# Half of the output weights split later, in places of the first expert's weights, and two more places for experts' tiles

## The chip, the cores and the metric

The kernel runs on one core of a Trainium2 chip (trn2). The metric is the device time of one execution in microseconds, lower is better. The time before is the median of three runs, 391.73 us (389.76 to 392.42).

## What is computed

Three stages follow one another, all in fp32 at the boundary.

```python
# retention: 8 batches, 8 heads, 576 positions, 64 wide; D[i,j] = gamma_h ** (i-j) for i >= j, else 0
x = (q @ k.T / 8 * D) @ v                       # -> x: 4608 tokens x 512
# soft mixture of experts: 8 experts of 4 slots; phi 512 x 32, w1[e] 512 x 1024, w2[e] 1024 x 512
logits = x @ phi
slots = softmax(logits, over tokens).T @ x      # 32 x 512
out_e = relu(slots[e] @ w1[e]) @ w2[e]          # 8 experts, 4 slots each
x = softmax(logits, over slots) @ out           # 4608 x 512
# bilinear block: m1, m2 512 x 1024; w3 1024 x 1024; w_out 1024 x 512
y = ((x @ m1) * (x @ m2)) @ w3 @ w_out          # 4608 x 512
```

The weights m1, m2, w3 and w_out come as float64 and are turned into fp32 on the chip; the rest is float32.

## The kernel before, in words

**The order of the work is written out by hand.** Each engine and each queue executes its instructions in the order in which the program emits them. All large loads go out on the sync queue (SP), in that order: a load whose place is still being read holds up every load that is written behind it.

**Attention** (0 to about 162 us) runs over 36 units of 128 tokens. Each unit multiplies queries, keys and values, scales, and turns the result for the expert logits. Beside it the loop loads what comes later. At three points of each unit `pace` lets one waiting load go, tied to an instruction of TensorE. The list of waiting loads holds key, value and query tiles and one `next_load` per unit (two in units 10, 14, 18, 22, 26). `next_load` takes the next *piece* of the float64 weights, if one of the four raw buffers is free, and otherwise calls `load_expert`, which takes the next expert tile if a place is free, and else does nothing. In the last nine units three more `load_expert` calls stand in each unit, and the places of keys, values and queries come free one after the other.

**Pieces.** There are 40 pieces of 512 KB: 8 of w_out (interleaved with the first of m1), 16 of m1 and m2, 16 of w3. Converting one takes two operations on ScalarE, three on VectorE and one addition on GpSimd (`conv_list`, `add`). A piece of w_out or w3 is then split into two fp32r numbers, high and low: a copy on ScalarE (`copy`, line 528) and a subtraction on GpSimd (`sub`, line 533). `nsplit` counts the splits. Values of w_out and w3 wait for the split in three buffers (`vals`).

**Products of w3 and w_out** (`emit_Ws`, line 564) are 64 groups of three 128x512 matmuls. Eight groups accumulate one block of 128 rows of w3 @ w_out; each group reads one of the eight split w_out pieces (`k8`), all of them in one tile, `wop`, of 32 KB per partition. The groups are used as filler for TensorE: three before the first expert, then as many at each of the four steps of an expert as a formula by step allows (line 956), 58 by the second step of the last one.

**Experts** (about 172 to 246 us). An expert's weights are eight tiles of 512 KB: four for the first layer (`emit_l1`, line 602), four for the second (`emit_l2`, line 622). Between the layers ScalarE applies the relu (607) and VectorE transposes (615). The places of a layer's four tiles go to the list `free` behind its matmuls, and `load_expert` (583) takes from it. In the first six experts one place per expert is kept for a finished block of w3 @ w_out (`wplaces`). With the experts' places and the ones that were in the attention 19 tiles are asked for before the first layer of the first expert: one place (`ew0`) is there for experts from the start, the other 18 come free during the attention's end. At the first expert `ew0` and one further place go to the softmax over slots.

**Behind the experts** come the slots' outputs through m1 and m2, the products of pairs of slots (written over the split w_out), the matmul of these with w3 @ w_out, and then nine token blocks with 12 matmuls for each 128 tokens and the stores.

Of the kernel before, what the change touches and what calls it, by code (L numbers as in the profile page):

```python
# [10 lines left out]
F32R = mybir.dt.float32r  # L11
# [5 lines left out]
ALU = mybir.AluOpType  # L17
# [14 lines left out]
def retention_softmoe_bilinear(  # L32
# [15 lines left out]
    nc = tc.nc  # L48
    const = ctx.enter_context(tc.tile_pool(name="const", bufs=1))
# [20 lines left out]
    bank = [*b2(scores), one, output[:, 512:1024], state, output[:, 0:512], *b2(pair)]  # L70
# [10 lines left out]
    block = lambda t, i, n=1: t[:, 1024 * i:1024 * (i + n)]  # L81

    mw_sb = const.tile([128, 8192], F32, name="mw_sb")
    wop = const.tile([128, 8192], F32R, name="wop")
    w3p = const.tile([128, 3072], F32R, name="w3p")

    NRAW = 4
# [10 lines left out]
    def place(tag, name=None, dt=F32):  # L98
        t = new("place", name or tag, 1024, dt, tag=tag)
        all_places.append((t, tag))  # L100
        return t

    def tag_of(t):
        return next(g for x, g in all_places if x is t)

    both = lambda t: [t[:, o:o + 512] for o in (0, 512)]
# [12 lines left out]
    xt_places = [place(f"xts{i}") for i in range(3)]  # L119
    xg_places, p_places, s_place, kt_place = [place("xg0"), place("xg1")], [place("pm0"), place("pm1")], place("st"), place("kt")  # L120
# [5 lines left out]
    qb = [place(f"q{i}") for i in range(QBUF)]  # L126
    vb = [place(f"v{i}") for i in range(VBUF)]
    rb = [place(f"kr{i}") for i in range(RBUF)]
    kb = [place(f"k{i}") for i in range(KBUF)]
    ring = [place("ew0")]  # L130


    lo, hi = slice(0, 64), slice(64, 128)
# [324 lines left out]


    pieces = []  # L460
    woh, wol = wop[:, 0:4096], wop[:, 4096:8192]
    for i in range(8):
        pieces.append(wo[:, 512 * i:512 * i + 512])
    for i in range(16):
# [2 lines left out]
        pieces.append(w3[i // 2][:, 512 * (i % 2):512 * (i % 2) + 512])  # L467
    N3 = 24
    turn = [j for i in range(8) for j in (i, 8 + i)] + list(range(16, len(pieces)))
    nth = lambda j: j if j < 8 else j - 16  # L470

    def value(j):
        t = mw_sb[:, 512 * (j - 8):] if 8 <= j < N3 else vals[:, 512 * (nth(j) % 3):]
        return t[:, 0:512]

# [37 lines left out]

    def high_low(j):
        if j < 8:
            return woh[:, 512 * j:512 * j + 512], wol[:, 512 * j:512 * j + 512]
        t = block(w3p, (j - N3) % 3)
        return t[:, 0:512], t[:, 512:1024]

    def add(i):  # L520
        j = turn[i]
        ti = value(j).bitcast(I32)
        nc.gpsimd.tensor_tensor(out=ti, in0=ti, in1=parts[i % 2].bitcast(I32), op=ALU.add)  # L523
        if not 8 <= j < N3:
            copies.append(j)

    def copy(j):
# [16 lines left out]
    nsplit, nW = [0], [0]  # L544
# [3 lines left out]
    wplaces = xg_places[:]  # L548
# [3 lines left out]
    def emit_Ws(n, lag=1):  # L552
        for _ in range(n):
            i, k = divmod(nW[0], 4)
            if i == 16 or nsplit[0] < min(9 + i + lag, 24):
                return
            nW[0] += 1
            ps = bank[(5, 2)[i // 2 % 2]]
            b = block(w3p, i % 3)
            ah, al = (b[:, o + 128 * k:o + 128 * k + 128] for o in (0, 512))  # L560
            k8 = 4 * (i % 2) + k
            bh, bl = (t[:, 512 * k8:512 * k8 + 512] for t in (woh, wol))
            for part, (x, y) in enumerate(((ah, bh), (ah, bl), (al, bh))):
                nc.tensor.matmul(out=ps, lhsT=x, rhs=y, start=(k8 == 0 and part == 0), stop=(k8 == 7 and part == 2))  # L564
            if k8 == 7:
                evicts.append(lambda cb=i // 2, ps=ps: evict(cb, ps))
# [9 lines left out]
    ew, free = [], []  # L576
# [41 lines left out]
    def emit_l2(e):  # L618
        ht = ht_of[e]
        for cb in range(8):  # L620
            qd = cb % 4
            nc.tensor.matmul(  # L622
                out=bank[4][32 * qd:32 * qd + 32], lhsT=ht[:, 32 * cb:32 * cb + 32], rhs=ew[8 * e + 4 + cb // 2][:, 512 * (cb % 2):512 * (cb % 2) + 512],
                start=(e == 0 and cb < 4), stop=(e == 7 and cb >= 4), skip_group_check=True,
            )
        free.extend(ew[8 * e + 4:8 * e + 8])
# [28 lines left out]
    with tc.manual_schedule():  # L655
# [69 lines left out]
        output_factors(0)  # L725
        output_factors(1)

        free.extend(ring)
        came, TWICE, PACED = [], (10, 14, 18, 22, 26), 3

        def can_conv():
            if nconv[0] == nl[0]:
                return False
            j = turn[nconv[0]]
            return 8 <= j < N3 or nth(j) < nsplit[0] + 3

        def next_conv(u):
            if not conv_ops and nconv[0] < len(came) and came[nconv[0]] <= u and can_conv():
# [11 lines left out]
        for u in range(NU):  # L750
# [32 lines left out]
            if u + 1 < NU:  # L783
                emit_state(u + 1)
                n = pairs_in_order.index(units[u + 1][0]) if units[u + 1][1] else 0
# [52 lines left out]
        run(subs)  # L838
        run_copies()
        run(adds)  # L840
        free.extend([*p_places, s_place])
        load_expert(4)
        load_pieces()
        close_pool("psum")
# [19 lines left out]
        emit_dT(T)  # L864
        emit_xtr(NU - 2)
        emit_xtr(NU - 1, nc.vector.tensor_copy)
        free.extend(xt_places)
        load_expert(7)
        nc.tensor.matmul(out=bank[1][:, 0:1], lhsT=nrow.rearrange("p g s -> p (g s)"), rhs=ident[0:1, 0:1], start=True, stop=True)
        negm = tmp.tile([128, 1], F32, tag="negm", name="negm")  # L870
# [12 lines left out]
        for k in range(4):  # L883
            for a, b in ((lo, 64), (hi, 0)) if k % 2 else ((slice(0, 128), 0),):
                n = a.stop - a.start
# [7 lines left out]
            out=sme, in0=sT.rearrange("p k (e j) -> p e k j", j=4),  # L893
            in1=rzs.rearrange("p x (e j) -> p e x j", j=4).to_broadcast([128, 8, 4, 4]), op=ALU.mult,
# [25 lines left out]
            run(evicts)  # L920


        nsoft = [0]

        def soft():
# [12 lines left out]
        for e in range(NE):  # L938
            load_expert(8)
            last = emit_l1(e)  # L940
            if e == NE - 1:
                store_expt(last)
            if e == 0:

                free[:] = [t for t in free if not any(t is x for x in ring)]
                second = tag_of(free.pop(0))
                etp = [place("ew0", "et0"), place(second, "et1")]
                L["et"] = [t.rearrange("p (t n) -> p t n", n=128) for t in etp]
                L["soft"] = [etp[1][:, o:o + 128].rearrange("p (g s) -> p g s", g=4) for o in (512, 640)]
            for t in range(4):  # L950
                tick()
                if t == 1:
                    emit_turned(e)
                load_expert(8)
                step = 4 * e + t + 1
                emit_Ws(max(0, (min(5, 3 + step), min(7, 1 + step), min(55, 7 + (step - 8) * 48 // 20))[min(e, 2)] - nW[0]))
                if e == NE - 1 and t == 1:
                    emit_Ws(3, 0)
                if t == 2:
                    emit_l2(e)  # L960
                    if len(wplaces) < 8:
                        wplaces.append(free.pop(0))
                    load_expert(8)
                while e < NE - 1 and nsoft[0] <= (4 * e + t) * 18 // 28:
                    soft()
                convert(3)
# [12 lines left out]

        m4 = lambda t: t.rearrange("p (m n) -> p m n", m=4)  # L980
        two = lambda tag, n: [t[:, o:o + 512] for t in [place(tag, n, F32R)] for o in (0, 512)]
        left = [t for t in map(tag_of, qb + vb + rb + kb + p_places + [s_place, kt_place] + xt_places) if t not in [second, *map(tag_of, wplaces)]]
        cs2 = two(left[0], "cs")
        for i in range(2):
            L["cc"].append(tuple(zip(*[two(t, f"cc{i}{m}") for m, t in enumerate(left[4 * i + 1:4 * i + 5])])) + (cs2[i],))
# [1 line left out]
        gs, phl = two(left[10], "gs")  # L987
        phl = phl.rearrange("p (c x s) -> p c x s", c=8, x=2)
        y16 = [vals[:, 512 * i:512 * i + 512] for i in range(2)]
        ph, pl = (wop[:, 4096 * i:4096 * i + 4096].rearrange("p (c n) -> p c n", c=8) for i in range(2))  # L990
        ab = [t.rearrange("p (c s) -> p c s", c=8) for t in (mw_sb[:, 3584:4096], parts[0])]
        af = bank[4].rearrange("p (c s) -> p c s", c=8)
        for x in range(2):
            mw = mw_sb[:, 4096 * x:4096 * x + 4096].rearrange("p (k f) -> p k f", k=4)
            for k in range(4):
                for g in range(4):
                    nc.tensor.matmul(
                        out=bank[7 - x][32 * g:32 * g + 32, 0:256], lhsT=sot[:, k],
# [35 lines left out]
        def pairs(cb):  # L1034
            if cb > 7:
                return
            t1, t2 = sums(cb), ptmp[cb % 2][1]
            v = nc.vector
            for a, b in ((0, 4), (4, 8), (8, 16)) if cb == 0 else ((0, 16),):
                c = max(a, 1)  # L1040
                v.tensor_tensor(out=t2[:, c - 1:b - 1], in0=base(ab[1], cb, b - c), in1=win(af, cb, c, b - c), op=ALU.mult)
                v.tensor_tensor(out=t1[:, a:b], in0=base(af, cb, b - a), in1=win(ab[1], cb, a, b - a), op=ALU.mult)
                v.tensor_tensor(out=t1[:, c:b], in0=t1[:, c:b], in1=t2[:, c - 1:b - 1], op=ALU.add)
                nc.scalar.copy(out=ph[:, cb, 32 * a:32 * b], in_=t1[:, a:b].rearrange("p a b -> p (a b)"))

        def pairs_low(cb):
            t1 = sums(cb).rearrange("p a b -> p (a b)")
            nc.vector.tensor_tensor(out=pl[:, cb, 0:512], in0=t1, in1=ph[:, cb, 0:512], op=ALU.subtract)

        GB = (0, 1, 5, 3)  # L1050

        def g_mm(cb, m, parts):
            sl = slice(128 * m, 128 * m + 128)
            for i in parts:
                a, b = ((ph, wh), (ph, wl), (pl, wh))[i]
                nc.tensor.matmul(
                    out=bank[GB[m]], lhsT=a[:, cb, sl], rhs=b[cb],
                    start=(cb == 0 and i == 0), stop=(cb == 7 and i == 2), skip_group_check=True,
                )

# [154 lines left out]
```

## Time and profile before

| | |
|---|---|
| median of three runs | 391.73 us (389.76 to 392.42) |
| the profiled execution's own time | 393.84 us |
| its span | 392.1 us |
| TensorE matmul busy | 375.4 us (96%) |
| TensorE weight loads busy | 284.9 us (73%) |
| VectorE busy | 257.4 us (66%) |
| ScalarE busy | 199.0 us (51%) |
| GpSimd busy | 172.6 us (44%) |
| moved by the sync queue's transfers | 107.85 MB, 86.4% of 16 engines' span |
| read from memory | 97.41 MB |

Matmuls are pipelined: a 128x512 matmul is shown with about 0.40 us, but in a row of them the next one starts long before the one ahead ends. So "busy" says that TensorE has something in flight, and not that it works at its best. PE is TensorE's matmul row, PEld its weight-load row, DVE VectorE, ACT ScalarE, POOL GpSimd, SPq the sync queue. Tiles of experts' weights are named by the place that they are in (`k`, `kr`, `q`, `v`, `xts`, `ew`), so `xts<-in_ew` is a load of expert weights into a place that held something else before. Where several instructions stand in one row, its duration is from the first start to the last end.

### The profile page before, as it was taken

How to read it: one execution, taken by the hardware profiler on the slowest of the kernel's cores; microseconds unless marked ns; L12 is line 12 of the kernel's file. 1: busy time of each engine (PE TensorE's matmuls, PEld its weight loads, DVE VectorE, ACT ScalarE, POOL GpSimd, SP SyncE). 2: the span in 40 equal slices, each digit the busy share in tenths (PEclk: the TensorE clock that was granted, in tenths of full speed). 3: DMA queues.
4: the chain of work that ended last, by engine and by line, in shares of the span. 5: the costliest groups of instructions: out<-in, count | busy, mean ns of one | idle time of the engine just before them, and what ended most of it. 6: DMA issues, size and time to landing. Idle time of an engine off the chain costs nothing.

```text
span 392.1 us, 10958 instructions
## 1 busy us (share of the span) xinstructions
PE 375.4 (96%) x4447; PEld 284.9 (73%) x4447; DVE 257.4 (66%) x432; ACT 199.0 (51%) x424; POOL 172.6 (44%) x158
## 2 busy tenths in 40 slices
PE   6999999999997999799999999999999999999996
PEld 3888787878876897564666664678688777788774
DVE  4648999899896889555477963399766445355500
ACT  2347696788675787423364532234445353544432
POOL 2733765675464436202345652127544334552420
PEclk9999999999999999999999999999999999999999
DMA  7999899899988999999999999692359989998634
GB/s 241 335 331 333 301 365 323 252 375 376 291 274 313 305 324 331 325 397 371 410 409 408 410 407 389 153 210 39 82 114 207 232 221 227 235 222 210 158 89 103
DMA packets 48211, 108.75 MB, mean 277 GB/s; under 512 B 7584, under 2 KB 10016, under 8 KB 48160
## 3 DMA queue, kind: packets, MB, share of 16 engines
q1 hardware_dynamic: 47008, 107.85, 86.4%
q8 instruction: 35, 0.57, 0.6%
q10 hardware_dynamic: 1152, 0.20, 0.3%
q14 instruction: 16, 0.13, 0.1%
HBM read 97.41 MB, written 10.62 MB: 275 GB/s over the span
## 4 chain that ended last, share of the span: by engine, by line
PE 74%; DVE 14%; DMA 8%; issue 2%; ACT 1%; POOL 1%; ACTq 0%; POOLq 0%; DVEq 0%
PE bank L564 10%; PE bank L1131 9%; PE bank L1133 8%; PE bank L1132 8%; PE output L282 6%; PE scores L253 5%; DMA kr<-in_v 4%; PE output L316 4%; PE bank L622 3%; PE bank L602 3%; PE state L296 3%; DMA v<-in_ew 2%; PE one L356 2%; PE bank L1122 2%; PE pair L215 2%; DVE vals L497 2%
## 5 line engine op out<-in xcount | busy, mean ns | idle before, releaser
L646 POOL TENSOR_TENSOR cc<-mw_sb,cc 128x512 fp32r<-128x512 f32 x36 | 46.0, 1297 | 56.5 <-ACT cc L645 56.5
L523 POOL TENSOR_TENSOR vals<-vals,msb 128x512 int32<-128x512 int32 x24 | 30.8, 1284 | 46.7 <-DVE vals L497 44.5
L564 PE MATMUL bank<-wop,w3p 128*128 128x512 f32 x192 | 50.0, 404 | 0.0
L263 DVE TENSOR_TENSOR pm<-scores,msb 128x1024 f32<-128x1024 f32 x31 | 37.8, 1220 | 15.0 <-PE scores L253 14.8
L564 PEld LDWEIGHTS bank<-wop,w3p 128*128 128x128 f32 x192 | 34.4, 188 | 14.4 <-issue 7.1
L645 ACT CAST cc<-mw_sb 128x512 fp32r<-128x512 f32 x36 | 22.2, 616 | 43.6 <-DVE mw_sb L644 34.8
L1131 PE MATMUL bank<-w3p,cc 128*128 128x512 f32 x108 | 43.1, 399 | 0.0
L1133 PE MATMUL bank<-w3p,cc 128*128 128x512 f32 x108 | 42.1, 390 | 0.0
L1132 PE MATMUL bank<-w3p,cc 128*128 128x512 f32 x108 | 42.0, 389 | 0.0
L253 PE MATMUL scores<-q,kt 64*128 64x128 f32 x496 | 36.6, 285 | 2.0 <-issue 2.0
L644 DVE TENSOR_TENSOR mw_sb<-lga,raw 128x512 f32<-128x512 f32 x32 | 29.3, 955 | 12.3 <-POOL cc L646 12.1
L282 PE MATMUL output<-pm,v 128*64 128x128 f32 x512 | 36.1, 284 | 1.0 <-issue 1.0
L523 POOL TENSOR_TENSOR mw_sb<-mw_sb,msb 128x512 int32<-128x512 int32 x16 | 20.4, 1276 | 33.9 <-DVE mw_sb L497 25.7
L1135 ACT ACTIVATE mw_sb<-bank,rz 128x512 f32<-128x512 f32 x36 | 24.7, 685 | 19.0 <-PE bank L1133 9.4
L253 PEld LDWEIGHTS scores<-q,kt 64*128 64x128 f32 x496 | 30.3, 187 | 4.8 <-issue 2.9
L533 POOL TENSOR_TENSOR w3p<-vals,w3p 128x512 fp32r<-128x512 f32 x16 | 21.2, 1326 | 28.7 <-ACT w3p L528 19.8
L282 PEld LDWEIGHTS output<-pm,v 128*64 128x64 f32 x512 | 28.1, 139 | 6.1 <-issue 4.9
L220 ACT COPY kt<-pair 128x512 f32<-128x512 f32 x26 | 15.2, 585 | 29.1 <-PE pair L219 29.1
L504 ACT ACTIVATE msb<-raw 128x512 int32<-128x512 uint32 x40 | 27.8, 696 | 0.0
L192 POOL TENSOR_TENSOR k<-kr,msb 128x512 f32<-128x512 f32 (+1 forms) x30 | 25.9, 886 | 3.9 <-DMA kr<-in_v 3.9
L1131 PEld LDWEIGHTS bank<-w3p,cc 128*128 128x128 f32 x108 | 20.3, 188 | 7.1 <-issue 2.9
L503 DVE TENSOR_SCALAR vals<-vals 128x512 f32<-128x512 f32 x24 | 18.5, 772 | 7.6 <-ACT vals L502 7.6
(226 smaller groups left out, 775.3 us busy)
## 6 DMA issues: line engine op xcount, KB each, us to landing
q<-in_q SPq DMA_DIRECT2D x20, 512.0 KB, 6.5
raw<-expt SPq DMA_DIRECT2D x36, 256.0 KB, 4.4
kr<-in_v SPq DMA_DIRECT2D x16, 512.0 KB, 6.0
v<-in_v SPq DMA_DIRECT2D x16, 512.0 KB, 6.8
raw<-in_m SPq DMA_DIRECT2D x16, 512.0 KB, 6.2
raw<-in_w SPq DMA_DIRECT2D x16, 512.0 KB, 6.1
out_x<-mw_sb SPq DMA_DIRECT2D x64, 128.0 KB, 2.4
q<-in_ew SPq DMA_DIRECT2D x14, 512.0 KB, 10.1
```

What stands on the lines that cost most here:

```text
L192: (nc.vector if first else nc.gpsimd).tensor_tensor(out=Ks[:, :, 0:m, h], in0=K[:, 1 - h, :, 0:m], in1=ktab(c, h)[:, 0:m].unsqueeze(1).uns ...
L253: last = nc.tensor.matmul(out=ps[:, p], lhsT=ktb[u % 2][a, p], rhs=Q[a, :, x, p], start=True, stop=True)
L263: nc.vector.tensor_tensor(out=p_places[u % 2].rearrange("p (g t) -> p g t", g=8), in0=(pair if u == 1 else scores).rearrange("p (g t) -> p ...
L282: last = nc.tensor.matmul(out=xt_view(p)[side(p, h)], lhsT=v_tile(u)[:, 1 - h, x, p], rhs=p_main(u)[:, h, p], start=(block_of(u) == 0 and ...
L504: lambda: nc.scalar.activation(out=p.bitcast(I32), in_=lo, func=ACTF.Copy, scale=2.0 ** -29),
L523: nc.gpsimd.tensor_tensor(out=ti, in0=ti, in1=parts[i % 2].bitcast(I32), op=ALU.add)
L564: nc.tensor.matmul(out=ps, lhsT=x, rhs=y, start=(k8 == 0 and part == 0), stop=(k8 == 7 and part == 2))
L644: eng.tensor_tensor(out=e, in0=x, in1=y[:, m], op=ALU.mult)
L646: nc.gpsimd.tensor_tensor(out=cl[m], in0=e, in1=ch[m], op=ALU.subtract)
L1131: nc.tensor.matmul(out=ob, lhsT=ch[m][:, sl], rhs=gh[m], start=False, stop=False)
L1132: nc.tensor.matmul(out=ob, lhsT=ch[m][:, sl], rhs=gl[m], start=False, stop=False)
L1133: nc.tensor.matmul(out=ob, lhsT=cl[m][:, sl], rhs=gh[m], start=False, stop=(m == 3))
```

## The change

The tile for the split w_out becomes half as large (four of the eight pieces), and the memory goes to four places: `ew1` and `ew2`, free for expert tiles from the start, and `wv0` and `wv1`, in which the converted but unsplit pieces 4 to 7 of w_out lie, two in each. These four pieces are not split in the attention. Behind the second layer of the first expert `split_late` takes the four places that this layer has just freed, and puts the split pieces there: four copies on ScalarE and four subtractions on GpSimd. `wv0` and `wv1` then join the list of free places. The formula for the products of w3 and w_out is changed: none in the first expert (three before it, as in the kernel before), up to six by the end of the second, then a slightly steeper line to the same 55 at the end of the seventh. One of the three places of the attention's turned outputs (`xt_places[0]`) joins the free list one call earlier. The rest of the diff follows from the eight pieces' being in several tiles.

```diff
-    wop = const.tile([128, 8192], F32R, name="wop")
+    wop = const.tile([128, 4096], F32R, name="wop")
...
     ring = [place("ew0")]
+    spare = [place("ew1"), place("ew2")]
+    wv_places = [place("wv0"), place("wv1")]
...
-    woh, wol = wop[:, 0:4096], wop[:, 4096:8192]
+    NWO = 4
+    nth = lambda j: j if j < 8 else j - 24 + NWO
+    wv = both(wv_places[0]) + both(wv_places[1])
+    wo_parts = [(wop[:, 1024 * i:1024 * i + 512], wop[:, 1024 * i + 512:1024 * i + 1024]) for i in range(NWO)]
...
-    nth = lambda j: j if j < 8 else j - 16
-
     def value(j):
+        if NWO <= j < 8:
+            return wv[j - NWO]
         t = mw_sb[:, 512 * (j - 8):] if 8 <= j < N3 else vals[:, 512 * (nth(j) % 3):]
...
     def high_low(j):
         if j < 8:
-            return woh[:, 512 * j:512 * j + 512], wol[:, 512 * j:512 * j + 512]
+            return wo_parts[j]
...
-        if not 8 <= j < N3:
+        if not NWO <= j < N3:
             copies.append(j)
...
-            if i == 16 or nsplit[0] < min(9 + i + lag, 24):
+            if i == 16 or nsplit[0] < min(NWO + 1 + i + lag, NWO + 16):
                 return
...
-            bh, bl = (t[:, 512 * k8:512 * k8 + 512] for t in (woh, wol))
+            bh, bl = wo_parts[k8]
...
-        free.extend(ring)
+        free.extend([*ring, *spare])
...
-            return 8 <= j < N3 or nth(j) < nsplit[0] + 3
+            return NWO <= j < N3 or nth(j) < nsplit[0] + 3
...
-        free.extend([*p_places, s_place])
+        free.extend([*p_places, s_place, xt_places[0]])
         load_expert(4)
...
-        free.extend(xt_places)
+        free.extend(xt_places[1:])
         load_expert(7)
...
+        def split_late():
+            homes = [free.pop(0) for _ in range(8 - NWO)]
+            for j, t in enumerate(homes, NWO):
+                t = place(tag_of(t), f"wo{j}", F32R)
+                wo_parts.append((t[:, 0:512], t[:, 512:1024]))
+                nc.scalar.copy(out=wo_parts[j][0], in_=value(j))
+                nc.gpsimd.tensor_tensor(out=wo_parts[j][1], in0=value(j), in1=wo_parts[j][0], op=ALU.subtract)
+            free.extend(wv_places)
+            return homes
...
-                emit_Ws(max(0, (min(5, 3 + step), min(7, 1 + step), min(55, 7 + (step - 8) * 48 // 20))[min(e, 2)] - nW[0]))
+                emit_Ws(max(0, (3, min(6, step - 2), min(55, 6 + (step - 8) * 49 // 20))[min(e, 2)] - nW[0]))
...
                 if t == 2:
                     emit_l2(e)
+                    if e == 0:
+                        homes = split_late()
                     if len(wplaces) < 8:
                         wplaces.append(free.pop(0))
                     load_expert(8)
...
-        ph, pl = (wop[:, 4096 * i:4096 * i + 4096].rearrange("p (c n) -> p c n", c=8) for i in range(2))
+        ph, pl = zip(*wo_parts)
```

## Rows read from the trace of the kernel before

**Rows 1.** Busy time by window: us, PE, PEld, DVE, ACT, POOL, granted clock, DMA share, GB/s.
```profile
105.00:110.00 5.00, 5.00 (x110) 4.63 (x106) 4.60 (x10) 3.98 (x11) 3.03 (x3) 1.00 0.83 262
125.00:130.00 5.00, 4.40 (x60) 4.21 (x61) 3.37 (x5) 2.92 (x7) 1.98 (x3) 0.66 0.90 296
170.00:175.00 5.00, 5.00 (x55) 3.40 (x54) 1.92 (x6) 0.28 (x2) 0.00 (x0) 1.00 1.02 413
240.00:245.00 5.00, 5.00 (x41) 2.15 (x33) 1.14 (x2) 0.97 (x2) 0.00 (x0) 1.00 1.03 371
```

**Rows 2.** Chain that ended last: start, us, what (issue to landing for a DMA).
```profile
0.80 4.17 DMA kr<-in_v
...
235.85 9.50 DMA v<-in_ew
```

**Rows 3.** Waits of TensorE's weight loads, 172 to 246: us, times, longest.
```profile
PEld bank L622 <- DMA v<-in_ew: 1.2, 1, 1.2
PEld bank L622 <- DMA q<-in_ew: 0.7, 1, 0.7
```

**Rows 4.** Timeline of VectorE and GpSimd, 93 to 102: start, us, instruction.
```profile
93.30 0.68 DVE L327 TENSOR_TENSOR xts<-output,slotm 128x512 f32<-128x512 f32 x1
97.48 0.68 DVE L327 TENSOR_TENSOR xts<-output,slotm 128x512 f32<-128x512 f32 x1
98.95 1.28 POOL L533 TENSOR_TENSOR wop<-vals,wop 128x512 fp32r<-128x512 f32 x1
101.63 0.68 DVE L327 TENSOR_TENSOR xts<-output,slotm 128x512 f32<-128x512 f32 x1
```

**Rows 5.** Timeline of the sync queue, 160 to 183: start and us of issue.
```profile
165.82 2.78 SPq L583 DMA_DIRECT2D xts<-in_ew  x3
...
174.71 0.37 SPq L583 DMA_DIRECT2D kr<-in_ew  x1
...
178.54 0.38 SPq L583 DMA_DIRECT2D v<-in_ew  x1
...
182.88 0.54 SPq L583 DMA_DIRECT2D q<-in_ew  x1
```

**Rows 6.** Landing of tiles by window: xts 160:170, kr 173:176, v 176:180, q 180:190.
```profile
DMA to landing us min/median/max: 10.3/10.3/10.4
DMA to landing us min/median/max: 6.5/6.5/6.5
DMA to landing us min/median/max: 6.8/6.8/6.8
DMA to landing us min/median/max: 7.9/8.6/9.4
```

**Rows 7.** Waits of the sync queue, whole span: us in total, times, longest.
```profile
SPq L583 <- PE bank L602: 5.1, 3, 4.7
```

**Rows 8.** Timeline of all engines, 174 to 177: start, us, instruction.
```profile
174.58 1.66 PE L564 MATMUL bank<-wop,w3p 128*128 128x512 f32 x6
...
175.13 0.45 DVE L615 STREAM_TRANSPOSE ht<-hr 128x256 f32<-128x256 f32 x1 [0.99 <-ACT hr L607]
...
176.17 0.62 PE L622 MATMUL bank<-k,ht 128*32 128x512 f32 x2
```

**Rows 9.** Lines 528 and 533, 150 to 262: ns min/median/max, first and last start.
```profile
L528 ACT CAST w3p<-vals x13: 602/617/623, 175.3 to 236.2; 128x512 fp32r<-128x512 f32 x13
L533 POOL TENSOR_TENSOR w3p<-vals,w3p x14: 1279/1298/1474, 152.3 to 237.2; 128x512 fp32r<-128x512 f32 x14
```

**Rows 10.** DMA issues of the page: form, count, KB each, us to landing.
```profile
out_x<-mw_sb SPq DMA_DIRECT2D x64, 128.0 KB, 2.4
```

**Rows 11.** Waits of TensorE, 60 to 130: us in total, times, longest.
```profile
PE scores L253 <- issue: 2.0, 1, 2.0
PE output L282 <- issue: 1.0, 1, 1.0
```

More of the change, by code (lines that the diff above doesn't have):

```diff
@@ L981, in retention_softmoe_bilinear @@
         two = lambda tag, n: [t[:, o:o + 512] for t in [place(tag, n, F32R)] for o in (0, 512)]
-        left = [t for t in map(tag_of, qb + vb + rb + kb + p_places + [s_place, kt_place] + xt_places) if t not in [second, *map(tag_of, wplaces)]]
+        left = [t for t in map(tag_of, qb + vb + rb + kb + p_places + [s_place, kt_place] + xt_places + spare + wv_places) if t not in [second, *map(tag_of, homes), *map(tag_of, wplaces)]]
         cs2 = two(left[0], "cs")
@@ L1043, in pairs @@
                 v.tensor_tensor(out=t1[:, c:b], in0=t1[:, c:b], in1=t2[:, c - 1:b - 1], op=ALU.add)
-                nc.scalar.copy(out=ph[:, cb, 32 * a:32 * b], in_=t1[:, a:b].rearrange("p a b -> p (a b)"))
+                nc.scalar.copy(out=ph[cb][:, 32 * a:32 * b], in_=t1[:, a:b].rearrange("p a b -> p (a b)"))
         def pairs_low(cb):
             t1 = sums(cb).rearrange("p a b -> p (a b)")
-            nc.vector.tensor_tensor(out=pl[:, cb, 0:512], in0=t1, in1=ph[:, cb, 0:512], op=ALU.subtract)
+            nc.vector.tensor_tensor(out=pl[cb], in0=t1, in1=ph[cb], op=ALU.subtract)
         GB = (0, 1, 5, 3)
@@ L1056, in g_mm @@
                 nc.tensor.matmul(
-                    out=bank[GB[m]], lhsT=a[:, cb, sl], rhs=b[cb],
+                    out=bank[GB[m]], lhsT=a[cb][:, sl], rhs=b[cb],
                     start=(cb == 0 and i == 0), stop=(cb == 7 and i == 2), skip_group_check=True,
```

## The prediction, made before the change was run

> **What bounds the kernel now.** I read the windows first, then the waits of TensorE and of the sync queue, then single stretches. The busy times by window [rows 1] say where the transfers have room: at 105 to 110 us the DMA share is 0.83, in the experts' stretch 1.02 to 1.03 with 371 to 413 GB/s. So the attention has holes in its transfers, and from about 165 us until the last expert tile is in (chain of waits: issued at 235.85, 9.50 us under way, there at 245.35 [rows 2]) it is one full queue. TensorE is nearly as full over that stretch. Its weight loads, which wait in its place, wait for an expert tile 1.2 and 0.7 us [rows 3], both at the very end, in the second layer of the last expert; other waits there are a few tenths each. So an expert tile that comes earlier can give back at most 1.9 us unless TensorE gets less to do, and it gets nothing less to do.
>
> **What the change does to the loads.** Two more places take expert tiles from the start. In the attention a load slot goes to a piece while one of four raw buffers is free, and otherwise to an expert tile. Units 10, 14, 18, 22 and 26 have two load slots, so a later slot finds no raw buffer. Following the lists: unit 15 gave tile 0 to the one place there was, and the same lack comes at units 19 and 23, where the old kernel had no place. The new one loads tiles 1 and 2 there, at about 94 and 111 us (a unit is about 4.15 us [rows 4]). From unit 28 on the load slots are the same as before, each with a tile number higher by two. By the first expert's start 21 tiles are asked for rather than 19.
>
> That credit is two tiles. In the full stretch a transfer of 512 KB takes its turn each 1.294 us: the last tile of the four behind the second expert's first layer was issued at 182.88 and took 9.4 us, so it was there at 192.3 [rows 5, 6]; from there to 245.35 come 36 tiles and 5 pieces, 41 transfers in 53.05 us. The credit is worth 2.59 us.
>
> **What it takes back.** The four tiles freed by the first expert's second layer are not reloaded: they become the homes of output weights 4 to 7. In exchange two places come free, of which one goes to a product and one (wv1) to tile 23. That load must wait until ScalarE has copied and GpSimd has subtracted all four pieces, because pieces 6 and 7 lie in wv1. Loads go out in the order written: behind it on the sync queue stand the four tiles of the second expert's first layer, and then everything else. The same line already held the queue for up to 4.7 us on TensorE [rows 7]. The Trainium skill, "DMA: Bandwidth & Descriptors", Anatomy of one DMA, says that a semaphore wait is on the issuing sequencer and the DMA engines only drain what they have; by that rule the change opens a hole, and the row agrees.
>
> When is wv1 free? The second layer waits for the transposed hidden values, ready at 175.13 + 0.45 = 175.58 [rows 8]; without the six products that stood before it, it starts at about 175.7 instead of 176.17. Its first two tiles are done about 1.1 us later (estimate: two rounds, each of 0.62 [rows 8] and partly over each other), then 0.62 for the first copy [rows 9], 0.13 to the next engine (estimate), and four subtractions at 1.30 [rows 9]: 175.7 + 1.1 + 0.62 + 0.13 + 5.2 = 182.8. The other three copies run beside the subtractions.
>
> What is the queue doing meanwhile? The third tile of 165.82 to 168.6 lands at about 178.6 (168.3 + 10.3), tile 20 of the old count at 174.71 + 6.5 = 181.2, and tile 23, issued at 178.54, at 185.3 [rows 5, 6]. In the new kernel what was asked for before 168.6 lands at the same time (the two extra ones long before), the two tiles behind the first layer at 179.9 and 181.2, and then nothing is queued until 182.9.
>
> How long does a tile take from an empty queue? The trace has none in this stretch. From below: a 128 KB store takes 2.4 [rows 10], with 384 KB more at 410 GB/s 3.4. From above: the first tile of the kernel took 4.17 with others started beside it [rows 2]. I take 3.6, nearer the store, since nothing else is under way. The skill's same section fits a fixed 2.0 us plus bytes over 436 GB/s, for another issuing path: 3.2, an estimate, and by it the end would be 0.4 us earlier than in the sum below.
>
> Sum for the transfers: tile 23 lands at 182.9 + 3.6 = 186.5, tile 27 four turns later at 191.7 (before: 192.3, but with one piece in between). The piece moved behind comes later, so 36 tiles and 6 pieces remain: 42 x 1.294 = 54.3. The last tile is there at 246.0 instead of 245.35: **+0.7 us**. With 3.4 or 4.17 it is +0.5 or +1.3; each us that wv1 is free later adds one.
>
> Sum for TensorE: the six products that covered ScalarE's and VectorE's turn in the first expert (174.58 to 176.17 [rows 8]) are done later; they cost 1.59 there and 0.47 of it comes back, so 1.1 us is a hole. In the second expert the first three are left as cover; I estimate 0.3 more. By the end of expert 6 the count of products is the same (55). 1.4 lost against 1.9 of waits for tiles: alone it would be ready 0.5 us earlier than before. The transfers, later by 0.7, end last.
>
> **The rest.** Four copies and four subtractions leave the attention. A unit with such a subtraction (97.48 to 101.63, subtraction at 98.95) takes 4.15 us, the one before without it 4.18 [rows 4]: nothing. I bound it by -2.4 (four times a 0.6 us copy) and zero. The two extra loads (units 19 and 23) push a values tile from unit 23 to 24, two units before it is wanted; other loads have three or four units. I take zero, and +2.6 (both in full) as the other end. Reordering the attention's last places changes one tile's place in a queue that is 10 us deep [rows 6]: zero, and the cover is that depth. The stages behind read the split weights from single tiles, in the same instructions.
>
> The profiled execution took 393.84 us, its span 392.1, 2.1 above the median of the runs; the sum is 393.84 + 0.7 for it, and 391.73 + 0.7 = **392.4 us** for the median.
>
> **Rivals.**
> (a) The queue does not run dry: the split is done before the backlog ends. For it: ScalarE and GpSimd are idle there. Against it: four subtractions in a row are 5.2 us and the backlog ends at 181.2. TensorE then decides, -0.5 (391.2), or -1.9 (389.8) if the hole of the first expert closes too. Chance 0.22.
> (b) Slower: the attention pays for the two tiles. A values tile that comes a unit later makes TensorE wait in unit 26; it decides from about 8 us of latency (two units), where 6 to 10 are seen [rows 6]. Price up to 2.6, and 0.7 remains: 395.0. Against it: the share of 0.83 near that load [rows 1]. Chance 0.12.
> (c) Slower: TensorE's clock falls behind the hole in the first expert. A stop of 1.0 us in the attention cost no clock, one of 2.0 us [rows 11] was followed by five us at a granted 0.66 [rows 1]. The levels being 1.2 and 2.4 GHz, that took 1.7 us; the same here makes TensorE end last at 391.73 - 0.5 + 1.7 = 392.9. My hole is 1.1, near the harmless one. The skill's "TensorE: Matmul & The Clock Gate", Part 1, has the clock released by activity and gated again by idling; the two stops agree. Chance 0.05.
> (d) That 2.0 us stop, which waits for nothing the trace shows, goes away or comes twice as the code shifts: up to 3.7 us with its clock, 388.7 or 396.1. Chance 0.09, evenly.
> (e) The change does not do what it says, since the two slots at units 19 and 23 go to pieces and the tiles come late, with the wait still there: 0.7 + 2.6, 395.0. Chance 0.04.
>
> **Numbers.** The forecast's own case has 0.48. Its bounds, +0.5 to +1.3, with the spread of three runs (389.76 to 392.42) laid around them, and (a) and most of (b), give **389.7 to 395.0**. Less than 1% (3.9 us) cannot be told from no change here. Faster by more needs (d) with (a): 0.06. Slower by more needs (b) or (e) with wv1 free two us late, or the bad side of (d): 0.08. Within: 0.86.
>
> **What would show it.** Right: two expert tiles issued near 94 and 111 us; tile 23 issued close behind the fourth subtraction at 182 to 184, nothing on the queue for some 2 us, a DMA share clearly under 1 around 182 to 186; the second layer of expert 0 before 176; the last tile landing near 246. Wrong: full transfers through 180 to 186 (then a); units 24 to 27 longer than 4.2 us (then b); a granted clock under 1 from 176 on (then c). The forecast falls if the last tile lands before 244 or after 248.

## The result, and the profile after

The changed kernel takes **393.93 us** (median of 21 runs, 392.04 to 397.73) against 391.73 for the kernel before (21 runs beside it): ratio 1.0056, interval 1.0034 to 1.0078, or 1.3 to 3.1 us more. The forecast was 392.4 (389.7 to 395.0): its sign was right, its size, +0.7, was a third of what came, +2.2.

Single spans mislead here: the profiled executions took 393.84 before and 393.11 after. The one of before has a 2.0 us stop of TensorE and a low clock in the attention [rows 1, 11]; after's longest such stop is 1.2 us and its clock stays at 1.00, so it reaches the experts 2.3 us sooner (170.40 for 172.72). I therefore compare **the stretch** from the first matmul of expert 0 to the first of the token blocks. TensorE's timeline shows both ends, of before:

```profile
172.72 0.64 PE L602 MATMUL bank<-ew,slotm 128*32 128x256 f32 x8
...
281.72 1.27 PE L1122 MATMUL bank<-gs,cs 64*128 64x512 f32 x4
```

and after:

```profile
170.40 1.50 PE L607 MATMUL bank<-ew,slotm 128*32 128x256 f32 x24
...
280.93 1.28 PE L1139 MATMUL bank<-gs,cs 64*128 64x512 f32 x4
```

The stretch was 281.72 - 172.72 = 109.00 us and is 110.53: **+1.53**. That lies in the interval of the ratio; from the token blocks on the two are the same (110.4 and 110.5 us to the end). Times counted from the first matmul of expert 0 are called "at +x" below.

The sync queue after, issues (start, us; compare [rows 5]):

```profile
93.53 0.38 SPq L588 DMA_DIRECT2D ew<-in_ew  x1
...
110.94 0.38 SPq L588 DMA_DIRECT2D ew<-in_ew  x1
...
172.39 0.37 SPq L588 DMA_DIRECT2D kr<-in_ew  x1
180.16 0.33 SPq L588 DMA_DIRECT2D wv<-in_ew  x1
180.58 0.38 SPq L588 DMA_DIRECT2D kt<-in_ew  x1
181.05 0.38 SPq L588 DMA_DIRECT2D v<-in_ew  x1
181.53 0.38 SPq L588 DMA_DIRECT2D k<-in_ew  x1
182.00 1.12 SPq L588 DMA_DIRECT2D q<-in_ew  x2
```

Two early tiles go out where they were forecast. Between 172.39 and 180.16 nothing is issued. The timeline of all engines shows what the queue waits for (compare [rows 8]):

```profile
172.81 0.45 DVE L620 STREAM_TRANSPOSE ht<-hr 128x256 f32<-128x256 f32 x1 [0.99 <-ACT hr L612]
173.31 0.62 PE L627 MATMUL bank<-k,ht 128*32 128x512 f32 x2 [0.98 <-DVE ht L620]
...
174.41 2.18 ACT L933 CAST wo<-wv 128x512 fp32r<-128x512 f32 x4 [1.43 <-PE bank L627]
175.11 5.02 POOL L934 TENSOR_TENSOR wo<-wv,wo 128x512 fp32r<-128x512 f32 x4 [14.79 <-ACT wo L933]
```

GpSimd's fourth subtraction ends at 175.11 + 5.02 = 180.13, and wv1's load leaves 0.03 us behind it. The windows after (columns as in [rows 1]) show the hole, and that the queue is not full again before 186:

```profile
178.00:180.00 2.00, 2.00 (x15) 0.94 (x17) 1.90 (x5) 0.91 (x3) 2.00 (x2) 1.00 0.00 0
180.00:182.00 2.00, 2.00 (x18) 0.64 (x11) 0.64 (x3) 0.91 (x3) 1.36 (x2) 1.00 0.37 88
182.00:184.00 2.00, 2.00 (x34) 1.07 (x34) 1.76 (x7) 0.69 (x3) 0.00 (x0) 1.00 0.91 305
184.00:186.00 2.00, 2.00 (x10) 1.63 (x11) 0.39 (x1) 0.72 (x3) 1.29 (x1) 1.00 0.93 324
186.00:188.00 2.00, 2.00 (x10) 1.63 (x9) 1.05 (x3) 0.92 (x2) 1.29 (x1) 1.00 1.03 397
```

Issue to landing of the tiles issued at 180 to 182.5, first wv, then q:

```profile
DMA to landing us min/median/max: 4.1/4.1/4.1
DMA to landing us min/median/max: 8.7/8.7/8.7
```

The chain of waits of after names the last expert tile (compare [rows 2]):

```profile
234.94 9.62 DMA k<-in_ew
```

It lands at 244.56, at +74.16; in before at 245.35, at +72.63. That is 1.53 later, as much as the stretch is longer. The waits of TensorE's weight loads, 172 to 250 (compare [rows 3]):

```profile
PEld bank L627 <- DVE ht L620: 1.5, 1, 1.5
PEld bank L627 <- DMA k<-in_ew: 1.1, 1, 1.1
PEld bank L627 <- DMA v<-in_ew: 0.8, 1, 0.8
PEld bank L607 <- DMA v<-in_ew: 0.6, 1, 0.6
PEld bank L607 <- DMA ew<-in_ew: 0.4, 1, 0.4
```

The 1.5 us is the hole in expert 0, whose cover of two products (the six matmuls of [rows 8]) is gone; the tiles are awaited again at the end.

### The profile page after: what moved, and what is told of

Read it like the earlier page. It is cut to its first block, busy times and chain, and to the rows that moved or that the text cites. A ratio compares the mean times of both kernels' runs of the same rounds, so it can differ in the third digit from the quotient of the medians.

```text
span 391.4 us, 10965 instructions
## 1 busy us (share of the span) xinstructions
PE 375.1 (96%) x4447; PEld 283.5 (72%) x4447; DVE 252.8 (65%) x432; ACT 199.5 (51%) x424; POOL 172.2 (44%) x158
## 2 busy tenths in 40 slices
DMA packets 48211, 108.75 MB, mean 278 GB/s; under 512 B 7584, under 2 KB 10016, under 8 KB 48160
## 4 chain that ended last, share of the span: by engine, by line
PE 70%; DMA 12%; DVE 8%; POOL 4%; SPq 3%; ACT 2%; issue 2%; ACTq 0%; POOLq 0%; DVEq 0%
PE bank L1148 9%; PE bank L1150 8%; PE bank L1149 8%; PE bank L569 8%; PE scores L255 6%; PE output L284 6%; PE output L318 4%; PE bank L607 3%; PE state L298 3%; PE bank L627 3%; DMA v<-in_ew 3%; DMA kr<-in_v 3%; DMA k<-in_ew 2%; PE one L358 2%; PE pair L217 2%; DMA msb<-in_tabs 2%
## 5 line engine op out<-in xcount | busy, mean ns | idle before, releaser
L528 POOL TENSOR_TENSOR vals<-vals,msb 128x512 int32<-128x512 int32 x20 | 25.7, 1286 | 37.8 <-DVE vals L502 33.5
L569 PE MATMUL bank<-wop,w3p 128*128 128x512 f32 x96 | 26.0, 406 | 0.0
L569 PE MATMUL bank<-wo,w3p 128*128 128x512 f32 x96 | 25.8, 404 | 0.0
L1148 PEld LDWEIGHTS bank<-w3p,cc 128*128 128x128 f32 x108 | 20.3, 188 | 7.1 <-issue 2.9
L1150 PEld LDWEIGHTS bank<-w3p,cc 128*128 128x128 f32 x108 | 20.3, 188 | 4.4
```

The source lines that it names most:

```text
L1148: nc.tensor.matmul(out=ob, lhsT=ch[m][:, sl], rhs=gh[m], start=False, stop=False)
L1150: nc.tensor.matmul(out=ob, lhsT=cl[m][:, sl], rhs=gh[m], start=False, stop=(m == 3))
```

## The experiments

**The theory** is the prediction's: the load of wv1, which waits for the split, empties the queue, and the end is later by what the refill costs. **The rivals:** TensorE's lost cover is the loss; the attention pays for the early tiles; the early tiles are worth more or less than their turns. The arithmetic is the same in all of them (e6 does two subtractions twice); places, order and the filling with products differ. Ratios are to the kernel before, run beside each (its median was then 391.73 to 392.42), so rows are compared by their ratios and not by their medians.

| kernel | stretch, us | against before | median, us | ratio, interval |
|---|---|---|---|---|
| before | 109.00 | | 391.73 | |
| after | 110.53 | +1.53 | 393.93 | 1.0056, 1.0034 to 1.0078 |
| e1_late_free | 108.73 | -0.27 | 392.10 | 0.9991, 0.9960 to 1.0021 |
| e2_wv1_first | 109.96 | +0.96 | 392.44 | 1.0012, 0.9974 to 1.0050 |
| e3_spares_late | 110.58 | +1.58 | 393.65 | 1.0046, 1.0012 to 1.0080 |
| e4_before_new_fill | 109.36 | +0.36 | 392.48 | 1.0015, 0.9985 to 1.0045 |
| e5_late_free_cover | 114.73 | +5.73 | 397.10 | 1.0127, 1.0100 to 1.0154 |
| e6_sub_twice | 113.34 | +4.34 | 395.75 | 1.0092, 1.0062 to 1.0123 |
| e7_late_free_spares_late | 108.75 | -0.25 | 391.55 | 0.9986, 0.9969 to 1.0003 |
| e8_cover_hold | 108.64 | -0.36 | 391.99 | 0.9982, 0.9949 to 1.0014 |
| e9_cover_hold_early_spares | 107.70 | -1.30 | 390.89 | 0.9969, 0.9938 to 1.0001 |

Each stretch is of one profiled execution, and the medians do not resolve differences of a few tenths. The stretches repeat better than the medians: where the programs and their waits agree, TensorE's matmuls start within 0.01 to 0.02 us of each other (after and e1 up to +56, e1 and e7 to the end of the stretch).

**e1_late_free** lets the queue go on: the two wv places come free behind the second expert's first loads, so that no load in front of those waits for the split.

```diff
-            free.extend(wv_places)
             return homes
...
                 load_expert(8)
+                if e == 1 and t == 0:
+                    free.extend(wv_places)
...
-                    if len(wplaces) < 8:
+                    if e and len(wplaces) < 8:
```

> The changed kernel, but the two places that held the unsplit pieces join the free list only behind the loads of the second expert's first layer, so that no load waits for the split ahead of them (one place for a product is taken an expert later). Theory of the hole: those four tiles go out at about 176.3 to 177.5 us of the changed kernel's profile instead of 180.6 to 182, the queue never stands empty, the DMA share at 176 to 182 rises from about 0.4 to 1.0, the last expert tile is there 3 to 4 us earlier and TensorE then decides: the experts' stretch (first layer of expert 0 to the last second layer) 2.3 to 2.9 us shorter than in the changed kernel, so 391.0 to 391.6 us in the median, just under the kernel before. Theory of TensorE's cover (the loss is the hole in expert 0 and the products put off): the queue is no matter, 0 to 0.4 us shorter. Theory of the attention (it pays for the two tiles): the stretch shortens, but the total stays above the kernel before.

The stretch is 1.80 us shorter than after's, not quite the 2.3 to 2.9 expected. The hole is gone (windows; 180 to 182 is +8.1 to +10.1 here, where after's queue is dry):

```profile
176.00:178.00 2.00, 2.00 (x30) 0.84 (x26) 0.58 (x2) 2.00 (x5) 1.41 (x2) 1.00 1.04 416
178.00:180.00 2.00, 2.00 (x26) 1.13 (x19) 0.56 (x2) 0.82 (x4) 2.00 (x2) 1.00 0.97 320
180.00:182.00 2.00, 2.00 (x16) 0.73 (x19) 1.86 (x6) 0.79 (x2) 2.00 (x3) 1.00 0.97 336
```

and its last tile, issued at 232.46, lands 10.1 later, at +70.7, which is 2.0 us before that of the kernel before. No tile is awaited long at the end (0.3 us at most in the second layers); TensorE decides, and with its hole in expert 0 it gains only 0.27. Up to +56 its matmuls start as in after; what after loses behind that is waiting for tiles. So the wait of that one load carries the whole loss of the change.

**e6_sub_twice** turns the knob the other way: the subtractions of pieces 6 and 7 are done twice, with the same values, so that wv1 is free later.

```diff
                 nc.gpsimd.tensor_tensor(out=wo_parts[j][1], in0=value(j), in1=wo_parts[j][0], op=ALU.subtract)
+            for j in (6, 7):
+                nc.gpsimd.tensor_tensor(out=wo_parts[j][1], in0=value(j), in1=wo_parts[j][0], op=ALU.subtract)
             free.extend(wv_places)
```

> The changed kernel with the subtractions of pieces 6 and 7 done a second time before their place is reloaded: GpSimd holds the place 2.5 us longer, and nothing else is added to any path of TensorE, ScalarE or VectorE. Theory of the hole: each us of that wait is a us at the end, stretch 113.0 to 113.1 us instead of 110.53, median 396.4 us. Theory of TensorE's cover or of the attention: nothing changes, 110.5 us.

The load leaves at 183.17, at +12.23, that is 2.47 later than after's at +9.76, and the transfers stand still (issue, then windows):

```profile
183.17 0.33 SPq L588 DMA_DIRECT2D wv<-in_ew  x1
```

```profile
180.00:182.00 2.00, 2.00 (x18) 0.58 (x11) 1.18 (x3) 0.31 (x1) 2.00 (x3) 1.00 0.00 0
182.00:184.00 2.00, 2.00 (x31) 1.10 (x33) 0.00 (x0) 0.00 (x0) 2.00 (x2) 1.00 0.01 4
```

The last tile lands at 238.24 + 9.70 = 247.94, at +77.0, 2.8 later than after's. TensorE's matmuls start as in after up to +44.8 and fall behind from there on, where they wait for tiles. The stretch is 2.81 longer than after's: 2.81 / 2.47 = 1.14 us for each us of the wait. The ratios put e6 only some 1.4 us over after, with intervals that overlap, so this slope rests on the two profiled stretches. With e1 the runs show the mechanism from both sides.

**e2_wv1_first** splits pieces 6 and 7, which lie in wv1, ahead of 4 and 5.

```diff
                 wo_parts.append((t[:, 0:512], t[:, 512:1024]))
+            for j in (6, 7, 4, 5):
                 nc.scalar.copy(out=wo_parts[j][0], in_=value(j))
```

> The changed kernel with the four pieces split in the order 6, 7, 4, 5, so that the place reloaded next is free two subtractions (2.5 us) earlier; the work is the same. Theory of the hole: the load goes out at about 177.6 us instead of 180.16, and the last tile lands 2.0 to 2.5 us earlier; the experts' stretch is 1.8 to 2.5 us shorter, 391.5 to 392.1 us. Theory of TensorE's cover: no change, or up to 0.6 us longer, because the product of piece 4 waits for its subtraction (now the third).

The load leaves at 176.89, at +8.14, 1.6 us earlier than after's, and the last tile is no longer awaited. But the product that needs piece 4 comes before its subtraction now. TensorE's weight loads wait:

```profile
PEld bank L569 <- POOL wo L935: 1.3, 1, 1.3
```

From the second expert's second layer on TensorE is 1.2 us behind after, until after in its turn waits for tiles. So the stretch is only 0.57 shorter than after's, where 1.8 to 2.5 was expected: the wait was moved from the queue to TensorE.

**e3_spares_late** gives the two extra places to expert tiles only at the attention's end, so units 19 and 23 load none.

```diff
-        free.extend([*ring, *spare])
+        free.extend(ring)
...
-        free.extend([*p_places, s_place, xt_places[0]])
-        load_expert(4)
+        free.extend([*spare, *p_places, s_place, xt_places[0]])
+        load_expert(6)
```

> The changed kernel, but the two spare places take expert tiles only at the attention's end, with the other places there; the attention loads what it loaded before the change. Theory that the credit is real and the attention has room for it: the attention is as long as in the changed kernel, and the experts' stretch 2.6 us longer (two tiles of 1.29), 396.5 us. Theory that the attention pays in full: the attention is 2.6 us shorter and the total the same, 393.9 us. Between them the ratio says how much it pays.

A miss: I expected 2.6 us more, and the stretch is the same (110.58 against 110.53). The queue's backlog ends later (the tile ahead of wv1's lands at +11.0, after's at +8.1), but wv1's load leaves at 180.74, again at +9.76, and the refill starts there:

```profile
178.00:180.00 2.00, 2.00 (x16) 1.28 (x16) 1.36 (x5) 1.37 (x4) 2.00 (x3) 1.00 0.81 320
180.00:182.00 2.00, 2.00 (x17) 0.56 (x10) 1.23 (x3) 0.33 (x2) 1.95 (x2) 1.00 0.34 100
```

After's share is 0.00 in the window where this one's is 0.81. While a wait holds the queue, tiles that come earlier only make the hole longer. The ratio, 1.0046 without the early tiles against 1.0056 with them, shows no price of theirs in the attention either, within intervals of 0.0034 and 0.0022 to each side.

**e4_before_new_fill** is the kernel before with the new count of products per step, alone.

```diff
-emit_Ws(max(0, (min(5, 3 + step), min(7, 1 + step), min(55, 7 + (step - 8) * 48 // 20))[min(e, 2)] - nW[0]))
+emit_Ws(max(0, (3, min(6, step - 2), min(55, 6 + (step - 8) * 49 // 20))[min(e, 2)] - nW[0]))
```

> The kernel before with the changed formula for the products of w3 and w_out (none in expert 0, up to six by the end of expert 1), and nothing else: all loads and places as before. Theory of the hole: TensorE loses 1.1 to 1.8 us in the first two experts and gets it back from its 1.9 us of waits for tiles at the end; the experts' stretch and the total are as before within 0.3 us, 391.7 us. Theory of TensorE's cover: the loss of the change is here, 1.5 us longer, 393.2 us.

+0.36 us, between the two theories and near the first. TensorE has the same 1.5 us wait for the transposed values as after and is 1.05 us behind the kernel before at the last expert's second layer; 0.7 of that comes back, since its waits for tiles (0.5 the longest) are shorter than in [rows 3].

**e5_late_free_cover** is e1 with a fourth product as cover in expert 0.

```diff
-(3, min(6, step - 2), ...)
+(4, max(4, min(6, step - 2)), ...)
```

> The changed kernel with the two places freed behind the second expert's first loads (as in the run e1_late_free), and with the one product that needs no late piece done in expert 0, where TensorE waits 1.5 us for the transposed values. If TensorE decides once the hole in the transfers is closed, the wait falls to about 0.8 us and the experts' stretch (first layer of expert 0 to the first matmul of the token blocks: 109.00 us before, 110.53 changed, 108.73 in e1) becomes 108.0; the median is 0.7 us under e1_late_free and about 1 us under the kernel before. If the transfers decide there, it stays at 108.7.

The worst miss: 6.0 us longer than e1. The fourth product releases the split of one more piece of the third weights, and with it a conversion starts in expert 0, ahead of the transposition on VectorE. Its rows, and GpSimd's beside them:

```profile
178.32 1.37 DVE L510 TENSOR_SCALAR vals<-vals 128x512 uint32<-128x512 uint32 x1
179.72 1.63 DVE L502 SCALAR_TENSOR_TENSOR vals<-raw,vals 128x512 uint32<-128x512 uint32 x1
...
181.80 0.43 DVE L620 STREAM_TRANSPOSE ht<-hr 128x256 f32<-128x256 f32 x1
```

```profile
175.47 5.34 POOL L934 TENSOR_TENSOR wo<-wv,wo 128x512 fp32r<-128x512 f32 x4
```

Behind the two conversions on VectorE stand the differences (line 399) from which ScalarE makes `et`, which TensorE turns next. TensorE waits for it, and its clock falls (windows):

```profile
PEld bank L411 <- ACT et L400: 4.9, 1, 4.9
```

```profile
180.00:182.00 2.00, 0.00 (x0) 0.00 (x0) 1.97 (x4) 0.08 (x1) 1.31 (x2) 0.56 0.00 0
182.00:184.00 2.00, 1.72 (x5) 1.16 (x5) 1.57 (x7) 0.67 (x3) 0.77 (x1) 0.50 0.77 274
184.00:186.00 2.00, 2.00 (x13) 0.51 (x16) 0.79 (x4) 0.14 (x1) 0.00 (x0) 0.50 0.94 248
```

**e7_late_free_spares_late** is e1 and e3 together: is an early tile worth something once the hole is gone?

> As e1_late_free (no load waits for the split), and the two spare places take tiles only at the attention's end. In the changed kernel this made no difference (110.58 against 110.53 us), which I explain by the queue's standing empty later anyway. If so, it must make one here, where the queue does not stand empty: the last tile 2.6 us later; in e1_late_free it is there about 2.1 us before its matmuls end the line, so the stretch is 0.3 to 0.8 us longer than 108.73. If the early tiles are worth nothing for another reason, 108.7 us.

No: 108.75 against e1's 108.73, where I expected 0.3 to 0.8 more. TensorE decides in both.

**e8_cover_hold** is e7 with one more product as cover in expert 0 and the fifth and sixth one step sooner in expert 1, and the split that disturbed e5 held back.

```diff
-        while copies and (copies[0] < N3 + 3 or nW[0] >= 4 * (copies[0] - N3 - 2)):
+        while copies and (copies[0] < N3 + 3 or nW[0] >= max(5, 4 * (copies[0] - N3 - 2))):
...
-(3, min(6, step - 2), ...)
+(4, min(6, step - 1), ...)
```

> As e7_late_free_spares_late, with the one product that needs no late piece in expert 0 and the next two at the second and third step of expert 1 (four, five and six done instead of three, four, five, six), and the next split of w3 held back until five products are out, so that no conversion starts in expert 0: in e5_late_free_cover such a conversion stood in VectorE's queue beside GpSimd's four subtractions and TensorE waited 4.9 us for what was behind it. If TensorE decides in e7, its wait for the transposed values in expert 0 falls from 1.5 to about 0.8 us and one product less is put off: stretch 107.9 to 108.2 us against 108.75, median 0.7 us under e7_late_free_spares_late. If the transfers decide, 108.7 us.

e5's stop is gone, which bears out its cause: 6.1 us against e5, with the same four products in expert 0 (7.0 in e9, which also has e5's early tiles). But 108.64 is only 0.1 better than e7, where 0.6 to 0.9 was expected.

**e9_cover_hold_early_spares** is e8 with the early tiles back.

> As e8_cover_hold, but with the two spare places open to expert tiles from the start, as in the changed kernel. If the early tiles are worth something once neither the hole nor TensorE's wait is in the way, the stretch is shorter than in e8_cover_hold, by up to 0.7 us; if the queue is long enough without them, the same, 107.9 to 108.2 us.

The best of all: 107.70, 0.94 shorter than e8. In expert 0 TensorE waits 0.5 for the transposed values instead of after's 1.5:

```profile
PEld bank L627 <- DVE ht L620: 0.5, 1, 0.5
```

e8 and e9 run alike up to +56.8 and part only in expert 6, where VectorE's conversion of a late piece (line 508) starts at +58.96 in e8 and at +57.65 in e9, and with it the transposition behind it and TensorE's second layer come later. In e8 (from 174.20):

```profile
236.85 0.62 PE L627 MATMUL bank<-q,ht 128*32 128x512 f32 x2 [0.52 <-DVE ht L620]
```

and in e9 (from 169.08):

```profile
231.14 0.62 PE L627 MATMUL bank<-v,ht 128*32 128x512 f32 x2
```

The second layer starts at +62.65 in e8 and at +62.06 in e9, 0.6 apart; the rest comes at the last expert tile, which lands at +72.25 in e8 and at +70.92 in e9. With hole and cover mended, the early tiles are worth 0.9 us in this pair of profiled executions; with either unmended (e3, e7), nothing. The ratios of e8 and e9 differ by 0.0013 and do not resolve it. The median, 390.89, beats after's ratio clearly (0.9969 against 1.0056, intervals apart); against the kernel before the interval ends at 1.0001, so a gain there is likely and not proven.

## Why the prediction was right, and where its sizes were off

**The loads.** Right: two tiles at 93.53 and 110.94 (forecast 94 and 111).

**The wait on the queue.** Right, and the decisive step. wv1's load was forecast at 182.9, at +10.18, and left at +9.76: 0.42 early. The copies began 0.07 sooner, the step from the first copy to GpSimd was 0.05 shorter (0.70 from one start to the other, of which I had made 0.75), the four subtractions took 5.02 for 5.2, and 0.03 from the last of them to the load took the place of 0.15 that I had rounded up. The tile asked for last before the hole landed at 172.39 + 6.1 = 178.5, at +8.1 (forecast 181.2, +8.5).

**A tile from an empty queue.** 4.1 us, not 3.6: +0.5, inside the bounds (3.4 to 4.17) and nearer the kernel's first tile than the store that I leaned on; e2's load took 4.0. The Trainium skill, "DMA: Bandwidth & Descriptors", Anatomy of one DMA, gives a fit of 2.0 us plus bytes over 436 GB/s for another issuing path, by which an estimate for this tile is 3.2; the measurement decides.

**The turns behind it.** This is the term that was mis-sized: I let the full rate of 1.294 us set in at once. wv1 landed at 184.26 and the fourth tile behind it at 182.00 + 8.7 = 190.7: 6.4 us for four turns of which I had made 5.2, **+1.2**. The windows show it, 305 and 324 GB/s at 182 to 186 against some 400 in a full queue.

**The rest of the queue.** 190.7 to 244.56 is 53.86 us for the 42 transfers, 1.28 each; forecast 54.3, -0.4.

So the forecast's +0.7 becomes 0.7 - 0.42 + 0.5 + 1.2 - 0.4 = +1.6; measured +1.53. That is above the sum's own bounds (+0.5 to +1.3), and the median, 393.93, is above them even with the spread of the three runs added (391.73 + 1.3 + 0.7 = 393.7). The median lies in the range only because the range was drawn up to 395.0 for rival (b), of which no run shows anything. So the mechanism was right; that the number fell inside was in part luck. In before's clock the last tile came at 172.72 + 74.16 = 246.9 (forecast 246.0; it would have fallen beyond 248). Beside this, the median's +2.2 leaves some 0.7 us, inside its interval, for which no row stands; whether anything is there stays open.

**TensorE alone.** Forecast -0.5 (1.4 lost, 1.9 given back); e1, where tiles hardly matter, has -0.27. By the last expert's second layer it is 1.05 behind the kernel before (+71.51 for +70.46), and 1.3 comes back. The wait in expert 0 was 1.5 us for the weight loads and 0.98 between matmuls; forecast 1.1.

**The attention at no cost.** No run shows a price: line 327 on VectorE (329 after), my mark of a unit, starts at 110.55, 113.80 and 118.26 before and at 110.29, 113.54 and 118.00 after, the same steps of 3.25 and 4.46.

**The credit.** "The credit is worth 2.59 us" was wrong as a price of the tiles' coming early. It entered the sum only as a count of tiles left, which was right, but rival (e) was priced with it, and e3 shows that case at +1.58, not +3.3.

**Rivals.** (a), no dry queue, did not happen; e1 makes it happen, and there it ends where its own first price said, near -0.5. Its second price, -1.9 with the hole closed too, is approached by e9 (-1.30). (e) did not happen, since the two tiles left near 94 and 111 us. (b) has no support: after's ratio is 0.4 us over that of e3, which has no early tiles, and the intervals speak against a price of 2.6 us, though not against a small one. (c) did not happen: after's 1.5 us wait left the granted clock at 1.00; e5's, of 4.9 us, did not. (d) makes single spans differ, as said above, and not the medians by more than their intervals.

## What to carry to other kernels

On a queue that issues in order, a load into a place that an engine must first read out belongs behind the loads that are ready to go; here each us of its wait cost about 1.1 us at the end. When a full queue is emptied, price the refill too: the first tile's whole latency, 4.1 us here, and several slow turns, 1.2 us beyond the sum that takes the full rate at once. And tiles asked for early are worth nothing while a later wait empties the queue or TensorE decides; with both mended they were worth 0.9 us in one pair of profiled executions.

## What the hardware showed beyond that

**A refill is slow.** After an empty queue the four 512 KB tiles behind the first landed 1.6 us apart on the mean, against 1.28 in the full queue, though all five were issued within 2.3 us; in e2, e3 and e6 the same four came 1.5, 1.5 and 1.7 us apart. Why stays open. Slow turns stand also where no queue ran dry: 320 and 336 GB/s over 178 to 182 in e1, in its windows above, and in before the five transfers that landed behind 185.36 came 1.38 us apart.

**VectorE beside a burst of GpSimd.** In e5 two VectorE instructions took 1.37 and 1.63 us beside the four subtractions; the same lines take 0.43 and 0.69 elsewhere (after, 99.90 and 100.36). Both were held by 0.94 us, less than one subtraction of 1.3, and both ended just behind a subtraction: at 179.69 and 181.36, 0.28 and 0.55 us after the third and the fourth had ended (179.41 and 180.81). In e8 the second line took 1.68 beside a single subtraction and ended again 0.55 behind it (236.45 and 235.90). The transposition, beside GpSimd's next operation (181.50, 1.27 us), took its usual 0.43. The Trainium skill, "SBUF — State Buffer", SBUF: two separate sides, has a port pair that VectorE and GpSimd share as an exclusive lock, held for a whole instruction while the other blocks; it names VectorE's instructions with two inputs in SBUF or in a two-port mode for it. e5's and e8's rows agree.

**The clock.** In e5 TensorE's weight loads stood for 4.9 us (its matmuls for 4.45), followed by a granted 0.50, the lower level of 1.2 GHz, over 182 to 186; a stand of 1.5 us (0.98 for the matmuls) in after left it at 1.00. The Trainium skill, "TensorE: Matmul & The Clock Gate", Part 1, has the clock gated by idling; these two rows agree.
